# The out projection of the second two batches as seven block products per half of d_ff

## The chip, the cores and the metric

One core of one Trainium2 chip runs the whole program. The time is the device time of one launch in microseconds, the median of three runs. The work runs on five engines with instruction streams of their own: PE (matmul), DVE (elementwise with two inputs), ACT (activation, here mostly copies), POOL, and SP, which issues the DMAs.

## What is computed

Causal attention over 4 batches, 12 heads, 448 positions and head dimension 64, and then a gated product on its output:

```
x = attention(q, k, v).reshape(1792, 768)
a = x @ w_a                      # 768 x 1536
b = x @ w_b
out = (a * b) @ w_out            # 1536 x 768
```

## The kernel before

**Precision.** Every matmul operand of the gated product is split into a high part (rounded to the 4-byte matmul type) and a low part (the rest). A product of two blocks of 128 rows is three matmuls into one bank: high by high, low by high, high by low (`products`, line 629 in the profile). ACT makes the high parts (`copy`, line 284), DVE the low parts by a subtraction (`two_input`, line 300).

**Two passes.** `order` lists the work of two passes over two batches each (448 columns a batch). In the first pass, beside which the attention of batches 2 and 3 runs, every matrix goes plainly: 24 units of w_a and w_b and 12 of w_out. The second pass starts with six units `s` for the lower half of d_ff. One unit forms a 128-row block of a and of b for both batches with seven block products instead of eight, in the Winograd form of Strassen's scheme (`seven`): 7 products of 3 blocks of 3 matmuls, 63 in all. The block sums of x (T1 to T4, B11, B21, B22) lie in rooms that the attention has left (`make_rooms`), those of the weights come from `prepare_all`, four products ahead (`AHEAD`). The three PSUM banks `m` take turns; a product that adds to a bank waits until DVE or ACT has read the partial sum in it (u2, u3, c22, c21, c12 are such sums). The gated product of the unit is stored as a high and a low part in `g_hi` and `g_lo` (`part_g`).

After the six `s` units come six column blocks of w_out for this half of d_ff, for each of the two batches 6 blocks of 3 matmuls into one bank. The result of the first half is copied out of PSUM by ACT and stored to DRAM (`o_keep`); in the second half it is loaded back into an `acc` buffer, added by DVE, and stored to `out`. Then the same for the upper half of d_ff. The text calls the four stages S0, O0, S1 and O1, a unit of S by its number f = 0 to 5 in the half.

**Order.** A planner (`Plan.order`) walks a list of operations with estimated times and sets the order of every engine's stream before the program runs; among the operations that are ready on an engine it takes the one that was written first. At run time each engine keeps this order and waits on semaphores. SP's DMAs are one queue in this order.

Of the kernel before, what the change touches and what calls it, by code (L numbers as in the profile page):

```python
# [230 lines left out]
def causal_attention_then_gated_product(  # L231
# [15 lines left out]
    def sb(tag, n, shape, dt=F32):  # L247
        return plan.ring(tag, n, lambda i: sbuf.tile(shape, dt, tag=f"{tag}{i}", name=f"{tag}{i}"))
# [19 lines left out]

    v_buf = [const.tile([P, 4, 2, D], F32, name=f"v{i}") for i in range(NVB)]

# [4 lines left out]
    w_hi = const.tile([P, 18, P], F32R, name="w_hi")  # L275
    w_lo = const.tile([P, 18, P], F32R, name="w_lo")
    w_keep = [dram.tile([P, UW], F32, name=f"w_keep{u}") for u in range(NU)]
    x_keep = [[dram.tile([P, S], F32, name=f"x_keep{b}_{k}") for k in range(KT)] for b in range(2)]
# [43 lines left out]
    def convert_unit():  # L322
        u, t = w_64.pop(0)
        e, m, wt = sb("w_e", 2, [P, UW], U32), sb("w_m", 2, [P, UW], U32), sb("w_32", 3, [P, UW])

# [249 lines left out]

    raw_x = {}

# [67 lines left out]
    def convert_next():  # L645
        n = turned[0]
        turned[0] += 1
        if n < NU:
            plan.soonest = HOLD[0] + HOLD[1] * n if n <= LEAD[0] else 0.0
            convert_unit()  # L650
            plan.soonest = 0.0
            load_next()
        elif n < len(order):
            kind, f = order[n]
            if kind == "s" and f % HF == 0:
                weights[f] = [load_32(place["a"](f)), load_32(place["b"](f))]
                to_prepare[0] = prepare_all(f)
            elif kind == "o" and f >= 4:
                load_kept(in_turn[n])

    def split_next():
        n = parted[0]
        parted[0] += 1
        if n < len(order):
            kind, f = order[n]
            if kind != "s":
                split_unit()
            elif f % HF == 0:
                for _ in range(AHEAD):
                    next(to_prepare[0])  # L670

    weights, to_prepare, ready = {}, [None], []

    def prepare_all(f0):

        for f in range(f0, f0 + HF):
            a, b = weights[f]
            for i in range(7):
                if i in (0, 4):
                    if f + 1 < f0 + HF:  # L680
                        weights.setdefault(f + 1, []).append(load_32(place["ab"[i // 4]](f + 1)))
                    else:
                        load_kept(place["o"](2 * (i // 4) + f0 // HF))
# [22 lines left out]
    def seven(f, n):  # L706
# [11 lines left out]
        for i, (ps, name, first) in enumerate(plan_of):  # L718
            next(to_prepare[0], None)
            if order[n + 1][0] == "o" and i == 4:  # L720
                split_next()
            w = ready.pop(0)
# [6 lines left out]
            elif i == 1:  # L729
                u2 = sb("acc", 3, [P, S])  # L730
                added(u2, bank_b, s1)
# [3 lines left out]
            elif i == 3:  # L735
                u3 = sb("acc", 3, [P, S])
                added(u3, bank_b, s1)
# [8 lines left out]
            else:  # L746
                c12 = mid()
                added(c12, bank_c, u2)
                both(lambda: c12.t, lambda: c12.t, lambda: c22.t, ALU.mult, [c22], [c12])
                part_g(3, f, lambda: c12.t, c12)  # L750

    def uses():

        for n, (kind, f) in enumerate(order):
# [15 lines left out]
            if kind == "s":  # L770
                if order[n + 1][0] != "o":
                    split_next()
                seven(f, n)
                yield
                continue
# [150 lines left out]
```

## Time and profile before

| | us |
|---|---|
| median of 3 runs | 645.51 |
| lowest and highest run | 645.36, 646.71 |
| the profiled execution | 646.08 |
| its span, first to last instruction | 644.3 |
| PE busy in the span | 636.1 (99%) |
| DVE, ACT, POOL busy | 454.9, 347.4, 46.9 |

Busy times of one engine add up the time in which at least one of its instructions was running. Matmuls overlap one another, so a busy PE is not a measure of its speed; the distance from one start to the next is. Columns and lines are explained with the rows below. A line number names the helper that recorded the operation, so operations are told apart by the names of their tiles: `m<-x_hi,w_hi` is a matmul into bank m that streams x_hi over weights w_hi, `w_lo<-w,w_hi` the low part of a weight.

### The profile page before, as it was taken

The numbers are of one execution on the slowest core, as the hardware profiler recorded it, in microseconds if no ns is written. First come the engines' busy times: TensorE is split into PE (matmuls) and PEld (weight loads), VectorE is DVE, ScalarE is ACT, GpSimd is POOL, SyncE is SP. The second block draws the span as 40 slices with busy tenths as digits, with TensorE's granted clock in tenths as the row PEclk, the third lists the DMA queues.
The fourth block names the chain that finished last, engine by engine and source line by source line (L and its number), as shares of the span: only waits on it lengthen the run. The fifth ranks groups of instructions, "written<-read, shape, count | busy, mean of one in ns | idle before, by whom it ended". The sixth has DMA issues, their size and how long they took to land.

```text
span 644.3 us, 11138 instructions
## 1 busy us (share of the span) xinstructions
PE 636.1 (99%) x4088; PEld 565.6 (88%) x4088; DVE 454.9 (71%) x1017; ACT 347.4 (54%) x826; POOL 46.9 (7%) x104
## 2 busy tenths in 40 slices
PE   9999999999999999999999999999999999999997
PEld 6666779899889889889889889999999999999996
DVE  6799988989697396498488587687861248886421
ACT  6988648578567666666765732444432334443100
POOL 3756320000000000000000000000000000000000
PEclk9999999999999999999999999999999999999999
DMA  8636645656737466355351375222233222223532
GB/s 293 210 107 201 198 150 191 222 190 211 254 124 282 164 237 223 107 187 189 120 182 61 106 234 188 63 74 61 63 92 128 92 86 70 58 66 93 159 126 89
DMA packets 41718, 95.88 MB, mean 149 GB/s; under 512 B 4800, under 2 KB 27840, under 8 KB 41664
## 3 DMA queue, kind: packets, MB, share of 16 engines
q1 hardware_dynamic: 41664, 95.18, 44.4%
q8 instruction: 32, 0.52, 0.3%
q14 instruction: 22, 0.18, 0.1%
HBM read 67.24 MB, written 27.92 MB: 148 GB/s over the span
## 4 chain that ended last, share of the span: by engine, by line
PE 89%; DVE 7%; ACT 1%; DMA 1%; POOL 0%; issue 0%; POOLq 0%; SPq 0%; DVEq 0%
PE m L629 75%; PE t L489 5%; PE s L438 3%; PE t L438 2%; PE pv L528 1%; PE pv L509 1%; PE m L528 1%; DVE early L447 1%; DVE p L447 1%; DVE pt L292 1%; ACT early L453 1%; DVE x_lo L300 1%; PE m L438 1%; DVE w_lo L300 1%; DMA w<-w_keep 1%; DVE w_e L344 0%
## 5 line engine op out<-in xcount | busy, mean ns | idle before, releaser
L629 PE MATMUL m<-x_hi,w_hi 128*128 128x448 f32 x432 | 160.0, 370 | 0.0
L629 PE MATMUL m<-x_lo,w_hi 128*128 128x448 f32 x432 | 156.5, 362 | 0.0
L629 PE MATMUL m<-x_hi,w_lo 128*128 128x448 f32 x432 | 156.5, 362 | 0.0
L629 PE MATMUL m<-g_hi,w_hi 128*128 128x448 f32 x288 | 105.2, 365 | 0.5 <-DVE mid L300 0.5
L629 PE MATMUL m<-g_hi,w_lo 128*128 128x448 f32 x288 | 104.4, 362 | 0.0
L629 PE MATMUL m<-g_lo,w_hi 128*128 128x448 f32 x288 | 104.3, 362 | 0.0
L300 DVE TENSOR_TENSOR w_lo<-w,w_hi 128x768 fp32r<-128x768 f32 (+1 forms) x84 | 66.3, 790 | 40.2 <-ACT w_hi L284 39.5
L629 PEld LDWEIGHTS m<-x_hi,w_hi 128*128 128x128 f32 x432 | 81.1, 188 | 5.9 <-issue 0.2
L629 PEld LDWEIGHTS m<-x_hi,w_lo 128*128 128x128 f32 x432 | 81.0, 188 | 5.5
L629 PEld LDWEIGHTS m<-x_lo,w_hi 128*128 128x128 f32 x432 | 81.2, 188 | 4.9
L284 ACT ACTIVATE mid<-m 128x448 f32<-128x448 f32 x72 | 39.1, 544 | 83.0 <-PE m L629 74.4
L284 ACT ACTIVATE w_hi<-w 128x768 fp32r<-128x768 f32 (+1 forms) x84 | 59.0, 703 | 41.9 <-PE m L629 27.5
L453 ACT ACTIVATE p<-p,st 128x448 f32<-128x448 f32 (+6 forms) x126 | 62.5, 498 | 32.5 <-DVE st L447 32.0
L300 DVE TENSOR_TENSOR mid<-m,acc 128x448 f32<-128x448 f32 x48 | 29.7, 622 | 42.3 <-PE m L629 41.4
L629 PEld LDWEIGHTS m<-g_hi,w_hi 128*128 128x128 f32 x288 | 53.9, 187 | 5.5 <-DVE mid L300 1.2
L629 PEld LDWEIGHTS m<-g_lo,w_hi 128*128 128x128 f32 x288 | 54.1, 188 | 3.7
L629 PEld LDWEIGHTS m<-g_hi,w_lo 128*128 128x128 f32 x288 | 54.0, 188 | 3.3
L284 ACT ACTIVATE pt<-t 128x512 f32<-128x512 f32 x72 | 40.7, 594 | 9.4 <-PE t L489 9.3
L284 ACT ACTIVATE g_hi<-mid 128x448 fp32r<-128x448 f32 x48 | 27.6, 575 | 32.9 <-DVE mid L300 32.9
L300 DVE TENSOR_TENSOR mid<-m,mid 128x448 f32<-128x448 f32 x36 | 22.4, 622 | 28.7 <-PE m L629 21.5
L344 DVE SCALAR_TENSOR_TENSOR w_e<-w,w_e 128x768 uint32<-128x768 uint32 x36 | 34.6, 962 | 7.5 <-ACT w_e L340 7.4
L340 ACT ACTIVATE w_e<-w_e 128x768 uint32<-128x768 uint32 x36 | 30.2, 844 | 13.3 <-DVE w_e L335 12.7
(95 smaller groups left out, 1037.6 us busy)
## 6 DMA issues: line engine op xcount, KB each, us to landing
w<-w SPq DMA_DIRECT2D x36, 768.0 KB, 4.5
w_keep<-w SPq DMA_DIRECT2D x36, 384.0 KB, 3.3
w<-w_keep SPq DMA_DIRECT2D x36, 384.0 KB, 3.1
raw<-qT SPq DMA_DIRECT2D x24, 224.0 KB, 4.1
raw<-kT SPq DMA_DIRECT2D x24, 224.0 KB, 4.3
o_keep<-mid SPq DMA_DIRECT2D x24, 224.0 KB, 2.0
acc<-o_keep SPq DMA_DIRECT2D x24, 224.0 KB, 2.8
out<-mid SPq DMA_DIRECT2D x24, 224.0 KB, 2.0
```

What stands on the lines that cost most here:

```text
L284: return nc.scalar.activation(o(), i(), AF.Copy)
L292: return nc.vector.tensor_copy(o(), i())
L300: plan.op(engine, ns, lambda: e.tensor_tensor(out=o(), in0=a(), in1=b(), op=op), reads, writes)
L340: plan.op("act", 840, lambda: nc.scalar.activation(e.t, e.t, AF.Copy, bias=-896.0 * 2**23, scale=8.0), [e], [e])
L344: plan.op("dve", 900, lambda: nc.vector.scalar_tensor_tensor(out=e.t, in0=high(), scalar=0x80000000, in1=e.t, op0=ALU.bitwise_and, op1=ALU ...
L438: x = nc.tensor.matmul(at[r][0].t[to * D:(to + 1) * D, at[r][1]], q[:, r * D:(r + 1) * D], k[:, 0:D * (r + 1)], start=True, stop=True)
L447: return nc.vector.tensor_tensor_reduce(out=view(r), in0=at[r][0].t[:, at[r][1]], in1=mask[:, S - n:], scale=-0.125, scalar=3.0e38, op0=AL ...
L453: return nc.scalar.activation(view(r), view(r), AF.Exp, bias=st.t[:, nm, r:r + 1], scale=-1.0, accum_out=st.t[:, sm, r:r + 1],)
L489: x = nc.tensor.matmul(t.t[:, P * i:P * (i + 1)], p.t[:, at:at + P], swapped if r in CROSSED else ident, is_transpose=True, start=True, st ...
L509: r = nc.tensor.matmul(ps.t[j * D:(j + 1) * D, 128 * c:S], vt.t[:, c, j, :], parts[n].t[:, j, o:o + count, :].rearrange("p i d -> p (i d)" ...
L528: r = nc.tensor.matmul((ps, more)[row].t[j * D:(j + 1) * D, D * k:S], vt.t[rows, c, j, :], parts[n].t[rows, j, o:o + NR - k, :].rearrange( ...
L629: r = nc.tensor.matmul(ps.t[:, :S], a[:, i, :], x(), start=first and n == 0, stop=last and n == 2, skip_group_check=part)
```

## The change

The two passes over d_ff of the second two batches now end in three units `oo` each instead of six blocks `o`. A unit takes two column blocks of w_out and both batches and forms the four results with seven block products of 3 blocks of 3 matmuls (`seven_out`). Its operand blocks are halves of g: B11 and B21 are the first and last three blocks of the first batch, T1 the difference of the batches in the first three, B22 the last three of the second batch, and T2, T3, T4 further differences. So `seven` now stores T1 in place of the second batch's g for f = 0 to 2, and for f = 3 to 5 forms T2, T3 and T4, with their high and low parts, in rooms `pt`, `v`, `w_m`, `acc` and `raw` (`sums_room`). For that `acc` gives up one of three buffers, and the weight sums of `prepare_all` both lie in `w_e`, one buffer each. `prepare_all` runs once, over all 18 units. Each of the products' partial sums has a bank of its own (`t0`, `t1`, `s0`, `s1`, `pv`). In the second half the results of the first are loaded into the rooms x_lo and x_hi of B11 and B21 in one block of twelve loads (`keep_rooms`), and added in place. The core of the diff:

```diff
-        more = [places("pt", 3, 1, 1024) for _ in range(1)]
+        more = places("pt", 3, 2, 1024)
         block["T2"] = [one[0:3], two[0:3]]
-        block["T4"] = [[one[3], two[3], *more[0]]]
+        block["T4"] = [[one[3], two[3], more[0]]]
+        spare.append(more[1])
...
         for h in range(2):
             for f in range(h * HF, (h + 1) * HF):
                 order += [("a", f), ("b", f)] if r == 0 else [("s", f)]
-            order += [("o", 2 * e + h) for e in range(ET)]
+            if r == 1:
+                order += [("oo", NP // 2 * h + j) for j in range(NP // 2)]
+            else:
+                order += [("o", 2 * e + h) for e in range(ET)]
...
+            if n == NU:
+                units = []
+                for h in range(2):
+                    units += [(place["a"](i), place["b"](i), False) for i in range(h * HF, (h + 1) * HF)]
+                    units += [(place["o"](4 * j + h), place["o"](4 * j + 2 + h), True) for j in range(NP // 2)]
+                weights.extend([load_32(u) for u in units[0][:2]])
+                to_prepare[0] = prepare_all(units)
...
                 if i == 0:
-                    s12, s34 = (plan.ring(tag, 2, lambda j, tag=tag: sbuf.tile([P, UW], F32, tag=f"{tag}{j}", name=f"{tag}_s{j}"))
-                                for tag in ("w_e", "w_m"))
+                    s12, s34 = (plan.ring("w_e", 2, lambda j: sbuf.tile([P, UW], F32, tag=f"w_e{j}", name=f"w_e_s{j}"))
+                                for _ in range(2))
...
-                t, at = ((a, lower), (s12, upper), (a, upper), (s34, lower), (s12, lower), (b, upper), (s34, upper))[i]
+                early_six = (a, lower), (s12, upper), (a, upper), (s34, lower), (s12, lower), (b, upper), (s34, upper)
+                t, at = early_six[(0, 4, 2, 1, 3, 5, 6)[i] if late else i]
...
-                u2 = sb("acc", 3, [P, S])
+                u2 = sb("acc", 2, [P, S])
                 added(u2, bank_b, s1)
...
-                u3 = sb("acc", 3, [P, S])
+                u3 = sb("acc", 2, [P, S])
                 added(u3, bank_b, s1)
...
                 added(c12, bank_c, u2)
-                both(lambda: c12.t, lambda: c12.t, lambda: c22.t, ALU.mult, [c22], [c12])
-                part_g(3, f, lambda: c12.t, c12)
+                if f % HF < 3:
+                    t = g_raw[f % HF] = sb("raw", 4, [P, 2, S])
+                    both(lambda: t.t[:, 1], lambda: c12.t, lambda: c22.t, ALU.mult, [c12, c22], [(t, 1)])
+                    both(lambda: t.t[:, 0], lambda: t.t[:, 1], lambda: c21.t, ALU.subtract, [(t, 1), c21], [(t, 0)])
+                    part_g(3, f, lambda: t.t[:, 0], (t, 0))
+                else:
+                    k = f % HF - 3
+                    t = g_raw[k]
+                    slots = sums_room(k)
+                    both(lambda: c12.t, lambda: c12.t, lambda: c22.t, ALU.mult, [c22], [c12])
+                    for name, i, x, y in (("T2", 0, c12, None), ("T3", 1, c12, None), ("T4", 0, c21, (t, 0))):
+                        both(lambda i=i: t.t[:, i], lambda x=x: x.t, lambda i=i: t.t[:, i], ALU.subtract, [x], [(t, i)])
+                        (hi, hi_key), (lo, lo_key) = sums[name, k] = slots.pop(0), slots.pop(0)
+                        copy("act", S, hi, lambda i=i: t.t[:, i], [(t, i)], [hi_key])
+                        two_input("dve", S, lo, lambda i=i: t.t[:, i], lambda hi=hi: hi().bitcast(F32), ALU.subtract,
+                                  [(t, i), hi_key], [lo_key])
+                    part_g(3, f, lambda: c12.t, c12)
...
+    def sums_room(k):
+        if not fixed:
+            spare.extend(x for _ in range(2) for x in places("pt", 3, 2, 1024))
+            spare.extend(x for _ in range(NVB) for x in places("v", NVB, 1, 512))
+            spare.extend(over("w_m", "", 2 * UW, plan.rings["w_m"][0]))
+            spare.extend(over("acc", 2, S, plan.rings["acc"][0][2:]))
+            plan.rings["acc"] = (plan.rings["acc"][0][:2], [0])
+            fixed.extend(spare)
+        return [fixed[0:6], fixed[6:8], fixed[8:12]][k] + [x for _ in range((0, 2, 1)[k]) for x in places("raw", 4, 2, 2 * S)]
...
+    def keep_rooms():
+        for n, tag in enumerate(("x_lo", "x_hi")):
+            x = plan.ring(tag, 2, lambda i, tag=tag: sbuf.tile([P, KT, S], F32, tag=f"{tag}{i}", name=f"{tag}_o{i}"))
+            for i in range(KT):
+                kept[i // 2 * 2 + n, 2 + i % 2] = (lambda x=x, i=i: x.t[:, i, :]), (x, i)
+        for e, b in sorted(kept):
+            o, key = kept[e, b]
+            load(P * S * 4, o, lambda b=b, e=e: o_keep[b][e], [("o", b, e)], [key])
...
+    def seven_out(j):
+        h, j = divmod(j, NP // 2)
+        if h and j == 0:
+            keep_rooms()
+        banks = {name: bank(tag) for name, tag in (("1", "t0"), ("5", "t1"), ("6", "s0"), ("7", "s1"), ("4", "pv"))}
+        places_of = tuple((e, b) for e in (2 * j, 2 * j + 1) for b in (2, 3))
...
+        s1, u2, u3 = of(sb("mid", 5, [P, S])), of(sb("acc", 2, [P, S])), of(sb("acc", 2, [P, S]))
+        o11, o12, o21, o22 = (kept[p] for p in places_of) if h else (of(sb("mid", 5, [P, S])) for _ in range(4))
+        plan_of = (("1", "B11", True), ("5", "T1", True), ("1", "B21", False), ("6", "T2", True),
+                   ("7", "T3", True), ("4", "T4", True), ("5", "B22", False))
+        for i, (ps, name, first) in enumerate(plan_of):
+            ps = banks[ps]
+            next(to_prepare[0], None)
+            w = ready.pop(0)
+            for k in range(3):
+                (hi, hi_key), (lo, lo_key) = part(name, k)
+                products(ps, w, k, hi, lo, first and k == 0, k == 2, [hi_key, lo_key], True)
+            ps = of(ps)
+            if i == 0:
+                copied(s1, ps)
+            elif i == 1:
+                add(o22, o22, ps) if h else copied(o22, ps)
+            elif i == 2:
+                add(o11, o11, ps) if h else copied(o11, ps)
+                store(o11, 0)
+            elif i == 3:
+                add(u2, ps, s1)
+                if h:
+                    add(o12, o12, u2)
+            elif i == 4:
+                add(u3, ps, u2)
+                if h:
+                    add(o21, o21, u3)
+                add(o22, o22, u3)
+                store(o22, 3)
+            elif i == 5:
+                add(o21, ps, o21 if h else u3)
+                store(o21, 2)
+            else:
+                add(o12, ps, o12 if h else u2)
+                store(o12, 1)
...
+                continue
+            if kind == "oo":
+                seven_out(f)
                 yield
                 continue
```

The order of the instructions, at three places. First DVE, at the border of units 3 and 4 of a half (f = 3, 4), from the add that forms c12 out of its bank up to and with the add into u2 (`acc`) of the next unit. Names: mid holds c11, c21, c22, c12 and s1; w_e_s and w_m_s are weight sums. Before:

```order
L300 TENSOR_TENSOR mid_4961<-m_4911,acc_4887 128x448
L300 TENSOR_TENSOR g_lo<-mid_4944,g_hi 128x448
L300 TENSOR_TENSOR mid_4961<-mid_4961,mid_4931 128x448
L300 TENSOR_TENSOR w_lo<-w_4815,w_hi 128x384
L300 TENSOR_TENSOR w_e_s_4954<-w_e_s_4954,w_4874 128x384
L300 TENSOR_TENSOR w_m_s_4987<-w_4874,w_4925 128x384
L300 TENSOR_TENSOR g_lo<-mid_4961,g_hi 128x448
L300 TENSOR_TENSOR acc_4997<-m_4972,mid_4976 128x448
```

and with the change:

```order
L301 TENSOR_TENSOR mid_4932<-m_4882,acc_4860 128x448
L301 TENSOR_TENSOR g_lo<-mid_4915,g_hi 128x448
L301 TENSOR_TENSOR mid_4932<-mid_4932,mid_4902 128x448
L301 TENSOR_TENSOR w_lo<-w_4784,w_hi 128x384
L301 TENSOR_TENSOR raw_4606<-mid_4932,raw_4606 128x448 x2
L301 TENSOR_TENSOR g_lo<-mid_4932,g_hi 128x448
L301 TENSOR_TENSOR pt_x_4967<-raw_4606,pt_x_4381 128x448
L301 TENSOR_TENSOR pt_x_4974<-raw_4606,pt_x_4967 128x448
L301 TENSOR_TENSOR raw_4606<-mid_4915,raw_4606 128x448
L301 TENSOR_TENSOR acc_4986<-m_4943,mid_4947 128x448
```

Seven operations stood ahead of the one into `acc`, with the first row; ten stand now (the row with x2 is two). The weight work that stood between them, but for one row, stands behind.

Second PE, from S0 to O0. Before, the stage O0 begins with the first batch's blocks in order, right behind the last product of S0:

```order
L629 MATMUL m_5123<-x_hi_4157,w_hi 128x448
L629 MATMUL m_5123<-x_lo_4168,w_hi 128x448
L629 MATMUL m_5123<-x_hi_4157,w_lo 128x448
L629 MATMUL m_5165<-g_hi,w_hi 128x448
L629 MATMUL m_5165<-g_lo,w_hi 128x448
L629 MATMUL m_5165<-g_hi,w_lo 128x448
```

With the change the first unit's T2, whose three blocks lie in pt, v and w_m, is taken in pieces with T3 (in pt, raw, w_m and acc), behind 9 matmuls of T1 and 9 of B21:

```order
L634 MATMUL s_5220<-v_x_5082,w_hi 128x448
L634 MATMUL s_5220<-v_x_5094,w_hi 128x448
L634 MATMUL s_5220<-v_x_5082,w_lo 128x448
L634 MATMUL s_5235<-pt_x_4967,w_hi 128x448
L634 MATMUL s_5235<-pt_x_4974,w_hi 128x448
L634 MATMUL s_5235<-pt_x_4967,w_lo 128x448
L634 MATMUL s_5220<-w_m_x,w_hi 128x448 x2
L634 MATMUL s_5220<-w_m_x,w_lo 128x448
L634 MATMUL s_5235<-raw_x_5092,w_hi 128x448 x2
L634 MATMUL s_5235<-raw_x_5092,w_lo 128x448
L634 MATMUL s_5235<-w_m_x,w_hi 128x448
L634 MATMUL s_5235<-acc_x,w_hi 128x448
```

A block of T3 (bank s_5235) stands ahead of the last block of T2, so that the sum which is made last is wanted three matmuls later. B11 stands even before T4 of the last unit of S0. Likewise at f = 4 and 5 six and nine matmuls of T1 now stand ahead of T3.

Third SP, before O1. Before:

```order
L303 DMA w_5983<-w_keep_107 128x768
L303 DMA acc_5995<-o_keep_0_140 128x448
L303 DMA w_6041<-w_keep_109 128x768
L303 DMA w_6082<-w_keep_111 128x768
L303 DMA acc_6096<-o_keep_1_141 128x448
L303 DMA w_6107<-w_keep_113 128x768
L303 DMA acc_6128<-o_keep_0_146 128x448
L303 DMA w_6143<-w_keep_115 128x768
```

and with the change:

```order
L304 DMA w_6112<-w_keep_110 128x768
L304 DMA x_lo_o_6138<-o_keep_0_141 128x448
L304 DMA x_lo_o_6138<-o_keep_0_147 128x448
...
L304 DMA x_hi_o_6141<-o_keep_5_152 128x448
L304 DMA w_6210<-w_keep_112 128x768
L304 DMA w_6245<-w_keep_114 128x768
```

The loads of the first half's results stood one by one between weights and stores; now the twelve stand in a block (ten in place of the dots), ahead of the last three weight loads.

## Rows read from the trace of the kernel before

**Rows 1.** Page, the span in 40 slices: busy tenths, granted clock.

```profile
PE   9999999999999999999999999999999999999997
...
PEclk9999999999999999999999999999999999999999
...
GB/s 293 210 107 201 198 150 191 222 190 211 254 124 282 164 237 223 107 187 189 120 182 61 106 234 188 63 74 61 63 92 128 92 86 70 58 66 93 159 126 89
```

**Rows 2.** Busy time by stretch (S0, O0, S1, O1); columns in the first line.

```profile
core 0: us, PE busy (x) PEld busy (x) DVE busy (x) ACT busy (x) POOL busy (x), PEclk, DMA share, GB/s
402.78:478.38 75.60, 75.60 (x380) 70.86 (x378) 56.55 (x106) 31.26 (x62) 0.00 (x0) 1.00 0.23 68
478.38:521.58 43.20, 43.20 (x218) 40.50 (x216) 12.87 (x21) 12.20 (x22) 0.00 (x0) 1.00 0.32 111
521.58:597.18 75.60, 75.60 (x380) 70.86 (x378) 56.03 (x105) 31.70 (x63) 0.00 (x0) 1.00 0.25 73
597.18:640.38 43.20, 43.20 (x217) 40.30 (x215) 12.84 (x19) 4.15 (x6) 0.00 (x0) 1.00 0.41 129
```

**Rows 3.** The chain that ended last, its last piece: start, us, what.

```profile
386.46 254.09 PE m L629 x1269
```

**Rows 4.** Timeline of PE, first matmul of S0, O0, O1: start, us, what.

```profile
402.78 0.36 PE L629 MATMUL m<-x_hi,w_hi 128*128 128x448 f32 x1
...
478.38 0.36 PE L629 MATMUL m<-g_hi,w_hi 128*128 128x448 f32 x1
...
597.18 0.36 PE L629 MATMUL m<-g_hi,w_hi 128*128 128x448 f32 x1
```

**Rows 5.** Timeline of all engines, the end.

```profile
640.18 0.37 PE L629 MATMUL m<-g_hi,w_lo 128*128 128x448 f32 x1
640.58 0.62 DVE L300 TENSOR_TENSOR mid<-m,acc 128x448 f32<-128x448 f32 x1 [2.98 <-PE m L629]
641.23 0.33 SPq L303 DMA_DIRECT2D out<-mid  x1
```

**Rows 6.** Timeline of DVE, inside S0; in brackets idle before and its releaser.

```profile
445.53 0.56 DVE L300 TENSOR_TENSOR w_lo<-w,w_hi 128x384 fp32r<-128x384 f32 x1
446.00 0.56 DVE L300 TENSOR_TENSOR w_m_s<-w,w_e_s 128x384 f32<-128x384 f32 x1
...
449.78 0.62 DVE L300 TENSOR_TENSOR mid<-m,acc 128x448 f32<-128x448 f32 x1 [0.71 <-PE m L629]
...
453.59 0.62 DVE L300 TENSOR_TENSOR mid<-m,acc 128x448 f32<-128x448 f32 x1
454.12 0.62 DVE L300 TENSOR_TENSOR g_lo<-mid,g_hi 128x448 fp32r<-128x448 f32 x1
454.66 0.62 DVE L300 TENSOR_TENSOR mid<-mid,mid 128x448 f32<-128x448 f32 x1
```

**Rows 7.** Timeline of DVE, start of O0.

```profile
480.19 0.95 DVE L300 TENSOR_TENSOR w_lo<-w,w_hi 128x768 fp32r<-128x768 f32 x1
481.06 0.62 DVE L300 TENSOR_TENSOR g_lo<-mid,g_hi 128x448 fp32r<-128x448 f32 x1
```

**Rows 8.** Timeline of ACT, inside S1.

```profile
561.38 0.55 ACT L284 ACTIVATE mid<-m 128x448 f32<-128x448 f32 x1 [0.95 <-PE m L629]
561.82 0.57 ACT L284 ACTIVATE g_hi<-mid 128x448 fp32r<-128x448 f32 x1
562.28 0.52 ACT L284 ACTIVATE w_hi<-w_m_s 128x384 fp32r<-128x384 f32 x1
```

**Rows 9.** Page, DMA issues: count, KB each, us to landing.

```profile
w<-w_keep SPq DMA_DIRECT2D x36, 384.0 KB, 3.1
...
acc<-o_keep SPq DMA_DIRECT2D x24, 224.0 KB, 2.8
```

**Rows 10.** Busy time by stretch near the start; columns as in rows 2.

```profile
10.00:15.00 5.00, 4.98 (x61) 3.23 (x65) 5.00 (x31) 4.73 (x20) 2.98 (x7) 1.00 0.98 341
15.00:20.00 5.00, 4.42 (x44) 3.00 (x37) 3.74 (x18) 4.81 (x18) 3.66 (x9) 1.00 1.03 392
```

More of the change, by code (lines that the diff above doesn't have):

```diff
@@ L267, in causal_attention_then_gated_product @@
     p_buf = [sbuf.tile([P, PW], F32, tag=f"p{i}", name=f"p{i}") for i in range(NPB)]
-    v_buf = [const.tile([P, 4, 2, D], F32, name=f"v{i}") for i in range(NVB)]
+    v_buf = [sbuf.tile([P, 4, 2, D], F32, tag=f"v{i}", name=f"v{i}") for i in range(NVB)]
     early = sbuf.tile([P, 2 * HF * S], F32, tag="g_hi", name="early")
@@ L276, in causal_attention_then_gated_product @@
     w_lo = const.tile([P, 18, P], F32R, name="w_lo")
+    w_m = sbuf.tile([P, 2, UW], U32, tag="w_m", name="w_m")
     w_keep = [dram.tile([P, UW], F32, name=f"w_keep{u}") for u in range(NU)]
@@ L323, in convert_unit @@
         u, t = w_64.pop(0)
-        e, m, wt = sb("w_e", 2, [P, UW], U32), sb("w_m", 2, [P, UW], U32), sb("w_32", 3, [P, UW])
+        e, m, wt = sb("w_e", 2, [P, UW], U32), plan.ring("w_m", 2, lambda i: w_m[:, i]), sb("w_32", 3, [P, UW])
         def low():
@@ L574, in split_block @@
         two_input("dve", S, lo, i, lambda: hi().bitcast(F32), ALU.subtract, [key, hi_key], [lo_key])
-    raw_x = {}
+    raw_x, spare = {}, []
     def both(o, a, b, op, reads, writes):
@@ L654, in convert_next @@
             kind, f = order[n]
[L655 to L659, printed above, removed]
+            if n == NU:
[5 more added lines that the diff above has]
+                to_prepare[0] = prepare_all(units)
     def split_next():
@@ L665, in split_next, with prepare_all @@
             kind, f = order[n]
-            if kind != "s":
+            if kind not in ("s", "oo"):
                 split_unit()
-            elif f % HF == 0:
+            elif kind == "s" and f == 0:
                 for _ in range(AHEAD):
                     next(to_prepare[0])
[L672 to L677, printed above, removed]
+    weights, to_prepare, ready = [], [None], []
+    def prepare_all(units):
+        for n, (_, _, late) in enumerate(units):
+            a, b = weights.pop(0), weights.pop(0)
             for i in range(7):
                 if i in (0, 4):
[L680 to L683, printed above, removed]
+                    if n + 1 < len(units):
+                        weights.append(load_32(units[n + 1][i // 4]))
                 if i == 0:
-                    s12, s34 = (plan.ring(tag, 2, lambda j, tag=tag: sbuf.tile([P, UW], F32, tag=f"{tag}{j}", name=f"{tag}_s{j}"))
-                                for tag in ("w_e", "w_m"))
+                    s12, s34 = (plan.ring("w_e", 2, lambda j: sbuf.tile([P, UW], F32, tag=f"w_e{j}", name=f"w_e_s{j}"))
+                                for _ in range(2))
                 lower, upper = slice(0, 384), slice(384, 768)
@@ L719, in seven @@
             next(to_prepare[0], None)
-            if order[n + 1][0] == "o" and i == 4:
-                split_next()
             w = ready.pop(0)
@@ new lines, in causal_attention_then_gated_product, with over @@
+    g_raw, sums, fixed = {}, {}, []
+    def over(tag, i, width, bufs):
+        t = Buf(lambda: sbuf.tile([P, width], F32R, tag=f"{tag}{i}", name=f"{tag}{i}_x"), [u for b in bufs for u in b.users])
+        for b in bufs:
+            b.live = False
+        return [((lambda c=c: t.t[:, c * S:(c + 1) * S]), (t, c)) for c in range(width // S)]
+    def sums_room(k):
[7 more added lines that the diff above has]
+        return [fixed[0:6], fixed[6:8], fixed[8:12]][k] + [x for _ in range((0, 2, 1)[k]) for x in places("raw", 4, 2, 2 * S)]
@@ new lines, in causal_attention_then_gated_product, with part, add, of @@
+    kept = {}
+    def keep_rooms():
[12 more added lines that the diff above has]
+        places_of = tuple((e, b) for e in (2 * j, 2 * j + 1) for b in (2, 3))
+        def part(name, k):
+            if name in ("T2", "T3", "T4"):
+                return sums[name, k]
+            b, i = {"B11": (0, k), "T1": (1, k), "B21": (0, k + 3), "B22": (1, k + 3)}[name]
+            return ((lambda: g_room.t[:, b, i, :]), ("g_hi", b, i)), ((lambda: g_lo[:, b, i, :]), ("g_lo", b, i))
+        def add(o, x, y):
+            (o, o_key), (x, x_key), (y, y_key) = o, x, y
+            both(o, x, y, ALU.add, [key for key in (x_key, y_key) if key is not o_key], [o_key])
+        def of(t):
+            return (lambda: t.t[:, :S]), t
+        def copied(o, x):
+            copy("act", S, o[0], x[0], [x[1]], [o[1]], True)
+        def store(o, n):
+            e, b = places_of[n]
+            load(P * S * 4, (lambda: out[b, e]) if h else (lambda: o_keep[b][e]), o[0], [o[1]], [] if h else [("o", b, e)])
+        s1, u2, u3 = of(sb("mid", 5, [P, S])), of(sb("acc", 2, [P, S])), of(sb("acc", 2, [P, S]))
[33 more added lines that the diff above has]
+                store(o12, 1)
@@ L773, in uses @@
                 seven(f, n)
+                yield
+                continue
+            if kind == "oo":
+                seven_out(f)
                 yield
```

## Prediction

> **What bounds the kernel now.** I read the 40 slices first, then the stages of the second two batches, then the chain that ended last. PE is busy in nine tenths or more of every slice but the last, at a full granted clock (1.00 in every stage of the table) [rows 1, 2]. That alone says little, since a matmul's 0.36 us overlaps its neighbours; the chain says more: its last piece is 254.09 us of nothing but 1269 matmuls, so 0.200 us each [rows 3]. The stage borders give the same: S0 starts at 402.78, O0 at 478.38, S1 at 521.58, O1 at 597.18, and the last slot ends at 640.38 [rows 2, 4, 5]. S0 and S1 take 75.60 us for 6x63 = 378 matmuls, O0 and O1 43.20 us for 12x18 = 216: exactly 0.200 us per matmul, no slot lost. From 402.78 on PE is the only bound, so a matmul less is 0.200 us less, as long as nothing else becomes late. What could is DVE: busy 56.55 of 75.60 us in S0 and 56.03 in S1, but 12.87 and 12.84 of 43.20 in O0 and O1; ACT has 31.26 of 75.60 at most [rows 2]. In S0 DVE's timeline has idle pieces such as the 0.71 us before 449.78, ended by PE's matmul [rows 6]: DVE waits for PE there, not PE for DVE.
>
> **What goes.** A pair of column blocks takes 4x18 = 72 matmuls before and 7x9 = 63 after. Three pairs in each half: 2 x (216 - 189) = 54 matmuls, 54 x 0.200 = **10.8 us**. The order of the changed kernel has the stages at 378 and 189. The shape stays (128x448 moving, 128x128 weights), so I take the same slot. The Trainium skill (TensorE: Matmul & The Clock Gate, "Back-to-back issue gap") has about 131 ns per matmul for a stream of weight load and matmul pairs at 512 columns. An estimate by that page is 54 x 0.131 = 7.1 us and an end near 638.4; the trace does not agree, with 0.200 us at 448 columns, and I give that case no chance worth carrying.
>
> **What is added, and its cover.** Start to start, a 128x448 DVE operation takes 0.53 to 0.54 us and a 128x384 one 0.47 [rows 6], a 768-wide one 0.87 [rows 7]; on ACT 0.44 and 0.46 [rows 8].
> - S units f = 0 to 2 of a half: one more subtraction, +0.53 us of DVE. Units 3 to 5: three subtractions and three lower parts, 6 x 0.535 = +3.2 us, and three ACT copies, +1.3 us.
> - O units: 7 lower parts and 4 sums of 384, 11 x 0.47 = 5.2 us a pair (before: two of 768, 1.7 us); adds of 448: 5 a pair in O0 where ACT's copies stood, 9 in O1 where 4 stood. A pair then needs 7.9 us of DVE in O0 and 10.0 in O1 out of 12.6 us of PE. Covered, with room.
> - ACT gains 18 copies of 448 and 42 of 384 in place of 12 of 768: under 60 x 0.46 = 27.6 us, over four stages in which it was busy for 79 of 237.6 us [rows 2]. Covered. POOL has no work here, before or after.
> - An S unit: 11 x 0.47 + 9 x 0.535 = 10.0 us of DVE now, 10.5 with f = 0 to 2, **13.2 with f = 3 to 5, where PE takes 12.6**. This is the one place where cover runs out. What matters is not the sum but which wait ends last, so I walked the new order there.
>
> Place A, the border of units 3 and 4, with t = 0 at the end of unit 3's last slot. A DVE add follows its slot's end by 0.2 us (640.38 to 640.58) [rows 5]. From the add into c12 to the add into u2 ten operations now stand, seven before: 9 x 0.535 + 0.47 = 5.3, so u2 starts at 5.5 and ends (0.62 long) at 6.1. Before, it waited for PE, at 3.8. T3 overwrites nothing until u2 has read the bank; in the new order six of T1's matmuls go ahead of it, so it needs the bank at 33 slots, 6.6 us. **0.4 us of room** with 0.1 for the signal. T4 then needs u3's read: DVE reaches it at 8.6, done at 9.2, and PE asks at 48 slots, 9.6. DVE is back on time within that unit, since the work it puts off is weights that are four products ahead. Unit 5 repeats it.
>
> Place B, from S to O, t = 0 at the end of unit 5. Nothing waits for the last products' sums until T2, since B11, T1 and B21 come first. c12 starts at 0.2; eight operations later the lower part of T2's third block starts at 4.3 and ends at 4.95; PE, which runs T3's first block ahead, asks for it at 28 slots, 5.6. T4's third lower part, six operations on, ends at 8.0; PE asks for it at 43 slots, 8.6. Again about 0.5 us of room. My count is good to about 0.5 us, so each of A (twice), B in both halves, six places, may cost 0 to 0.5: 0 to 3.0 us. I take **0.5** in all, nearer to nothing because in S and O of the kernel before no slot was lost, though DVE also answered within a microsecond of being needed.
>
> - SP's queue: 12 loads of the kept halves (224 KB, as the 12 loads into acc before) now stand in one block, behind B21's last read of the room and ahead of two weight loads (384 KB). 2.75 MB at 341 GB/s, the rate of the stretch 10 to 15 us that moved tiles of the same size [rows 10], is 8.1 us, plus 1.2 for the first weight load and about 2.8 to land [rows 9]: some 12 us after B21. The first DVE operation that needs that load stands behind u2 of O1's first pair, 45 + 30 slots, 15.0 us after B21. Cover 3 us. Without it DVE would stand still with u3 and the sums behind it, and PE's next bank reads wait: at the rate of the slice average (293 GB/s at best [rows 1]) cover is still 1.5 us. Cost 0.
> - The weight sums lose one of their two buffers each: a unit's s12 waits for the last one's readers, which are two or three products (1.8 us each) older. 0. The third acc buffer goes: u2 waits for c12's add, ahead of it on DVE anyway. 0.
> - Banks t, s and pv as accumulators, and rooms v, w_m, acc: not in the trace for these matmuls; the nearest rows are those of m banks and of rooms of the same kind, with the same slot [rows 3]. 0 on either side.
> - The end: one add, one store, 640.38 to 644.30, as before [rows 5]. 0.
>
> **Sum.** The profiled execution took 646.08 us, 644.30 of span and 1.78 around it. 646.08 - 10.8 + 0.5 = 635.8; the median of the three runs is 0.57 lower, so **635.2 us**. Without any stall 634.7.
>
> **Rivals.**
> - R1, DVE is the bound in units 3 to 5: 13.2 against 12.6, 0.6 x 6 = 3.6 us, if the queue cannot be carried past a unit. 645.5 - 10.8 + 3.6 = 638.3. For it: the sum is over. Against: some 2.6 us of idle DVE time (12.6 - 10.0) in each unit before, and O's DVE nearly empty. 0.13.
> - R2, the block of 12 loads is late by a few us and DVE holds PE once: 645.5 - 10.8 + 3 = 637.7. 0.03.
> - R3, slower: DVE's idle pieces cannot be filled, because its order fixes which add waits for which slot, and each added operation lands on PE's path. 2 x (3 x 0.53 + 3 x 3.2) = 22.4, end at 657.1. It decides from 12.1 us of added waits on, so over half of that work must be exposed. Against: in the order most added operations stand where DVE was waiting for PE. 0.03.
> - R4, slower too: the new waits bring PE's clock to its lower level (1.2 GHz). One O stage at that level costs 37.8 us more, end near 672. Against it: from 15 to 20 us PE is busy 4.42 of 5.00 us and is granted 1.00 [rows 10]. The Trainium skill (same page, "A second HAM failure mode: psum-queue depth-cycling") tells of a kernel in which short idles between groups of matmuls made the clock swing. By that rule this case would come; the trace, with the clock at 1.00 beside idles of that sort, does not bear it out. 0.01.
>
> **How the numbers follow.** My forecast has 0.79, and 0.01 is left for waits that eat just the gain. A measurement of this kernel can tell about 0.2% (1.3 us) from no change. Faster: 0.79 + 0.13 + 0.03 = 0.95; same 0.01; slower 0.03 + 0.01 = 0.04. The range runs from 633.9 (no stall, and the 0.8 that runs differ from one another) to 639.0 (R1 with the same noise).
>
> **What would show it.** PE should have 54 fewer matmuls, O0 and O1 37.8 us long, S0 and S1 75.6 to 77; PE waits on DVE under 1 us after 400 us; DVE in units 3 to 5 with hardly any idle time. R1 shows as PE waits on DVE in front of T3, T4 or the O stage's T2 to T4; R2 as DVE waiting for a load near 600 us; R4 as a granted clock below 1.00. Waits above 3 us in all would make the prediction wrong.

## Result and profile after

The changed kernel takes **636.58 us** (median of 4 runs, 634.85 to 637.46) beside 646.0 us for the kernel before on the same chip (4 runs, 645.36 to 646.71): ratio 0.9851, 95% interval [0.9826, 0.9876]. It is faster, by 9.4 us, inside the range of the prediction and 1.4 us above its number.

| | before | after |
|---|---|---|
| profiled execution, us | 646.08 | 637.46 |
| its span | 644.3 | 635.4 |
| PE busy (matmuls) | 636.1 (4088) | 625.8 (4034) |
| DVE busy (instructions) | 454.9 (1017) | 511.6 (1143) |
| ACT busy | 347.4 | 367.4 |
| S0 starts, last slot ends | 402.78, 640.38 | 403.85, 631.56 |

The page's slices of the changed kernel answer to [rows 1]: PE is full to the end as before, and the clock too.

```profile
PE   9999999999999999999999999999999999999997
...
DVE  6789988989777576598597597588899768889994
...
PEclk9999999999999999999999999999999999999999
```

Busy times by stretch of the changed kernel (S0, O0, S1, O1 and the tail; columns in the first line) answer to [rows 2]:

```profile
core 0: us, PE busy (x) PEld busy (x) DVE busy (x) ACT busy (x) POOL busy (x), PEclk, DMA share, GB/s
403.85:479.60 75.75, 75.75 (x380) 71.02 (x379) 66.01 (x129) 34.80 (x71) 0.00 (x0) 1.00 0.20 61
479.60:517.40 37.80, 37.80 (x191) 35.44 (x190) 31.67 (x62) 17.49 (x36) 0.00 (x0) 1.00 0.42 137
517.40:593.00 75.60, 75.60 (x380) 70.87 (x379) 65.96 (x129) 34.70 (x71) 0.00 (x0) 1.00 0.29 89
593.00:631.50 38.50, 37.87 (x190) 35.02 (x188) 32.85 (x63) 12.29 (x24) 0.00 (x0) 1.00 0.31 113
631.50:635.40 3.90, 0.23 (x2) 0.00 (x0) 0.62 (x1) 0.00 (x0) 0.00 (x0) 1.00 0.30 115
```

(The borders are cut by hand, 0.15 us behind the slot count. PE takes B11 of an O stage ahead of the last products of S, so an S stage has no clean end.) S0 and S1 last as long as before, with 9.5 and 9.9 us more DVE work in them. O0 has gone from 43.20 to 37.80. Only O1 is too long, with PE idle for 0.63 of its 38.50. After 395 us the view of PE's waits has a single row (waiting tile and line, its releaser: us in all, times, longest):

```profile
PE t L634 <- ACT mid L285: 0.6, 1, 0.6
```

The timeline of all engines in the changed kernel at that wait, in O1's second unit (start, us, what; in brackets the idle time before and its releaser):

```profile
607.05 0.37 PE L634 MATMUL t<-g_hi,w_lo 128*128 128x448 f32 x1
...
607.42 0.55 DVE L301 TENSOR_TENSOR w_e_s<-w,w 128x384 f32<-128x384 f32 x1
607.45 0.54 ACT L285 ACTIVATE mid<-t 128x448 f32<-128x448 f32 x1 [1.48 <-PE t L634]
607.88 0.55 DVE L301 TENSOR_TENSOR w_e_s<-w,w_e_s 128x384 f32<-128x384 f32 x1
...
608.05 0.47 PE L634 MATMUL t<-g_hi,w_hi 128*128 128x448 f32 x1 [0.64 <-ACT mid L285]
...
608.35 0.55 DVE L301 TENSOR_TENSOR w_lo<-w_e_s,w_hi 128x384 fp32r<-128x384 f32 x1
608.36 0.37 PE L634 MATMUL t<-g_lo,w_hi 128*128 128x448 f32 x1
...
608.56 0.36 PE L634 MATMUL t<-g_hi,w_lo 128*128 128x448 f32 x1
...
608.82 0.62 DVE L301 TENSOR_TENSOR x_lo_o<-t,x_lo_o 128x448 f32<-128x448 f32 x1
```

B11's last matmul starts at 607.05, and the next one is B21's first, into the same bank t0, so PE stands until ACT has copied B11 out. T1 doesn't go between them: its bank t1 still holds T1 + B22 of the unit before, which DVE reads only at 608.82, behind three operations on weights. Start to start the step costs 1.00 us in place of 0.20, and the one after it 0.31: 0.80 + 0.11 = **0.91 us**. (Here and below "lost" is the sum of such excesses over 0.200 per matmul, gaps over 0.05 us.)

The rest of the spans' difference lies ahead of S0, at the end of the first pass, which has the same instructions in the same order in both kernels. Two pieces of the changed kernel's chain that ended last, beside which [rows 3] has PE's last piece begin at 386.46:

```profile
380.78 4.18 DMA w<-w_keep
385.46 0.95 DVE w_lo L301
386.41 1.08 DVE mid L301 x2
387.54 88.48 PE m L634 x441
```

and the same place in the kernel before:

```profile
380.40 3.43 DMA w<-w_keep
...
385.29 1.13 DVE mid L300 x2
```

The wait for a weight load begins 0.38 us later in the chain and is 0.75 longer; two adds that free PE's bank stand behind it on DVE. That is 1.13 us, and S0 starts 1.07 later. The account of the spans, 644.3 to 635.4: -10.8 (54 slots) + 0.91 (O1) + 1.07 (before S0) - 0.08 (tail) = -8.9.

### The profile page after: what moved, and what is told of

It is laid out like the page before. It is cut to its first block, busy times and chain, and to the rows that moved or that the text cites. A ratio compares the mean times of both kernels' runs of the same rounds, so it can differ in the third digit from the quotient of the medians.

```text
span 635.4 us, 11232 instructions
## 1 busy us (share of the span) xinstructions
PE 625.8 (98%) x4034; PEld 555.5 (87%) x4034; DVE 511.6 (81%) x1143; ACT 367.4 (58%) x874; POOL 46.9 (7%) x104
## 4 chain that ended last, share of the span: by engine, by line
PE 87%; DVE 8%; DMA 2%; ACT 1%; issue 0%; POOL 0%; SPq 0%; POOLq 0%; DVEq 0%
PE m L634 61%; PE t L634 7%; PE t L490 5%; PE s L634 3%; PE s L439 3%; PE pv L634 2%; PE t L439 2%; PE pv L510 1%; PE pv L529 1%; PE m L529 1%; DVE early L448 1%; DVE p L448 1%; DVE pt L293 1%; ACT early L454 1%; DVE x_lo L301 1%; DMA acc<-o_keep 1%
## 5 line engine op out<-in xcount | busy, mean ns | idle before, releaser
L301 DVE TENSOR_TENSOR w_lo<-w,w_hi 128x384 fp32r<-128x384 f32 (+1 forms) x90 | 64.6, 719 | 13.1 <-ACT w_hi L285 12.8
L285 ACT ACTIVATE w_hi<-w 128x384 fp32r<-128x384 f32 (+1 forms) x90 | 58.2, 648 | 27.4 <-PE m L634 12.5
L285 ACT ACTIVATE w_hi<-w_e_s 128x384 fp32r<-128x384 f32 x72 | 37.3, 522 | 52.4 <-PE m L634 30.1
L285 ACT ACTIVATE mid<-m 128x448 f32<-128x448 f32 x60 | 32.6, 544 | 52.3 <-PE m L634 52.2
L634 PE MATMUL m<-g_hi,w_hi 128*128 128x448 f32 x144 | 53.4, 371 | 1.3 <-DVE mid L301 1.2
L634 PE MATMUL m<-g_hi,w_lo 128*128 128x448 f32 x144 | 52.1, 362 | 0.0
L634 PE MATMUL m<-g_lo,w_hi 128*128 128x448 f32 x144 | 52.1, 362 | 0.0
L301 DVE TENSOR_TENSOR w_lo<-w_e_s,w_hi 128x384 fp32r<-128x384 f32 x72 | 39.7, 552 | 11.4 <-ACT w_hi L285 10.3
L467 ACT ACTIVATE p<-p,st 128x64 f32<-128x64 f32 (+6 forms) x84 | 34.9, 497 | 1.0 <-DVE st L463 1.0
L343 DVE SCALAR_TENSOR_TENSOR w_m<-w_m,w 128x768 f32<-128x768 uint32 x36 | 34.4, 954 | 0.4
```

The costliest lines, as they stand in the source:

```text
L285: return nc.scalar.activation(o(), i(), AF.Copy)
L301: plan.op(engine, ns, lambda: e.tensor_tensor(out=o(), in0=a(), in1=b(), op=op), reads, writes)
L343: plan.op("dve", 900, lambda: nc.vector.scalar_tensor_tensor(out=r(), in0=m.t, scalar=2.0**32, in1=low(), op0=ALU.mult, op1=ALU.add), [m, ...
L467: return nc.scalar.activation(view(r), view(r), AF.Copy, scale=st.t[:, rc, r:r + 1])
L634: r = nc.tensor.matmul(ps.t[:, :S], a[:, i, :], x(), start=first and n == 0, stop=last and n == 2, skip_group_check=part)
```

## Experiments

Theories before the first of them. T: a slot is worth 0.200 us, the added work is covered with some tenths to spare, and what is missing is O1's wait plus a first pass that differs from run to run. R1: DVE is the bound, so its work shows in the time. R2: the block of kept loads costs something. Runs of the kernel before that a group shared: 644.91 us (644.36 to 645.7) for e1, e2, e5 and e7; 645.47 (645.06 to 647.61) for e3, e4 and e6; 645.91 (645.3 to 646.35) for e8.

### e1_again: the changed kernel, nothing edited

> The changed kernel once more, unaltered, for a tighter interval and a second profile. Theory: 54 matmul slots of 0.200 us are saved (10.8 us) and two waits give some back: 0.9 us in O1, where B21 of the second pair stands right behind B11 and waits for ACT's copy, in every run, and 0 to 1.5 us at the end of the first pass, where DVE waits for a weight load; so 9 to 10.5 us below the kernel before, S0 and S1 at 75.6. Rival (DVE is the bound in units 3 to 5): S0 or S1 longer than 76.5 us.

635.81 us (635.43 to 636.11), 9.10 under its kernel before, ratio 0.9859 [0.9842, 0.9875]. O1's wait is there again, 0.91 us at 606.02. S0 starts at 401.82, two microseconds earlier than in the first profile of the same program, and PE has no wait between 372 and 400 us. So the 1.07 us ahead of S0 is no cost of the change: this profile and those of the kernels below have S0 at 401.6 to 402.6, and e5, which is the kernel before with nothing added, has a wait of 0.5 us at the same place. Why that load lands when it does was not looked into.

### e2_banks: other banks for T1, B11, B21, B22

```diff
-        banks = {name: bank(tag) for name, tag in (("1", "t0"), ("5", "t1"), ("6", "s0"), ("7", "s1"), ("4", "pv"))}
+        banks = {name: bank(tag) for name, tag in (("1", f"t{j % 2}"), ("6", "s0"), ("7", "s1"), ("4", "pv"))}
+        banks["5"] = m_bank()
```

> The changed kernel, with the sums of B11+B21 alternating between banks t0 and t1 by pair and those of T1+B22 in the three m banks, so that no product of a pair has to wait for the last pair's bank. Theory (the wait in O1 comes from the turn of banks at the pair's border): O1 is 37.8 us with no wait, 0.9 us less than the changed kernel. Rival (DVE is too late in O1 whatever the bank): a wait of 0.5 us or more appears at another place of O1 and the time stays.

**634.36 us** (634.11 to 635.23), ratio 0.9837 [0.9822, 0.9852]: 10.55 under its kernel before and 1.45 under e1, whose runs all lie higher. PE loses nothing from S0 on; S0's start 401.62 and 1134 slots (2 x (378 + 189)) of 0.200 give the last slot's end, 628.42. Of the 1.45, 0.91 is the wait; the rest is within what runs differ by. This version beats both kernels; e3, e4, e6 and e7 start from it.

### e8_onebank: of that, T1's bank alone

```diff
-        ... (("1", "t0"), ("5", "t1"), ("6", "s0"), ("7", "s1"), ("4", "pv"))}
+        ... (("1", "t0"), ("6", "s0"), ("7", "s1"), ("4", "pv"))}
+        banks["5"] = m_bank()
```

> Edit: of the changed kernel, only the accumulator of T1 and B22 moves, from bank t1 to one of the three banks m; B11 and B21 keep t0. Theory (the wait in O1 came of bank t1 alone: its last sum is read late by DVE, so the order had to put B21 right behind B11): no wait of PE on ACT's copy out of bank t in O1, PE loses at most 0.2 us after 400 us, 634.4 like e2_banks. Rival (B11 and B21 sharing t0 is the cause): a wait of 0.5 us or more on ACT's copy stays in O1, 635.3 or more less what the end of the first pass gives or takes.

No wait is left, and nothing is lost from S0 on. The timeline of e8 at the place where the changed kernel stood (B11's last matmul, T1's first, ACT's copy of B11, B21's first):

```profile
605.55 0.36 PE L634 MATMUL t<-g_hi,w_lo 128*128 128x448 f32 x1
...
605.75 0.36 PE L634 MATMUL m<-g_hi,w_hi 128*128 128x448 f32 x1
...
605.95 0.55 ACT L285 ACTIVATE mid<-t 128x448 f32<-128x448 f32 x1 [1.48 <-PE t L634]
...
607.55 0.36 PE L634 MATMUL t<-g_hi,w_hi 128*128 128x448 f32 x1
```

With a turn of three banks T1 (bank m) goes between B11 and B21 again, nine slots of cover for ACT's copy. B11 and B21 still share t0, so that sharing was harmless by itself; bank t1's late reader was the cause. The median, 635.56 (634.81 to 636.1, ratio 0.9844 [0.9828, 0.9861]), is 10.35 under its own kernel before, near e2's 10.55. The number expected, 634.4, was that of e2 in another group; counted from each group's own kernel before, the two agree within the spread.

### e5_less: the kernel before with 54 matmuls left out

In O0 and O1 of the kernel before, one block product of three matmuls is left out in every column block of the first of the two batches and in half of those of the second, 18 block products in all; nothing is added.

```diff
+                        if first == 2 and k == 3 and (b == 2 or h == e % 2):
+                            yield
+                            continue
```

> The kernel before, with 54 of the 432 matmuls of O0 and O1 left out (one block of three in 9 of 12 column blocks and batches of each half), so its output is not the reference's; nothing is added. It is the price of the slots alone. Theory: 10.8 us below the kernel before, O0 and O1 37.8 us long. Rival (a matmul removed is worth 0.131 us): 7.1 us below.

634.47 us (634.04 to 635.73), ratio 0.984 [0.9825, 0.9854]: 10.44 less, 10.44 / 54 = 0.193 us for a matmul. The last piece of its chain:

```profile
385.79 243.30 PE m L629 x1215
```

That is 0.2002 each. e2, with all the added work, is as fast as this kernel, which has none of it: 634.36 and 634.47 in the same group. The estimate by the Trainium skill (TensorE: Matmul & The Clock Gate, "Back-to-back issue gap"), 0.131 us a matmul or 7.1 in all, is not borne out for this 448-column, 4-byte stream.

### e3_nosums: e2 without T1 to T4

The differences of g aren't formed; the four products read blocks of g that are there (B11's, B21's and B22's parts).

```diff
-                if f % HF < 3:
...
-                else:
...
-                    for name, i, x, y in (("T2", 0, c12, None), ("T3", 1, c12, None), ("T4", 0, c21, (t, 0))):
...
+                both(lambda: c12.t, lambda: c12.t, lambda: c22.t, ALU.mult, [c22], [c12])
+                part_g(3, f, lambda: c12.t, c12)
...
+            b, i = {"B11": (0, k), "T1": (1, k), "B21": (0, k + 3), "B22": (1, k + 3),
+                    "T2": (1, k + 3), "T3": (0, k + 3), "T4": (0, k)}[name]
```

> e2_banks without the block sums of g: T1 to T4 are not formed (no subtractions, no lower parts, no copies for them), and the seven products of O0 and O1 read blocks of g that are there anyway, so the output is not the reference's. PE's work is the same, DVE has 42 operations of 0.53 us less in S0 and S1. Theory (the added DVE work is covered): the same as e2_banks, 10.3 to 10.8 us below the kernel before. Rival (DVE is the bound in units 3 to 5): 3.6 us less than e2_banks.

634.72 us (633.76 to 635.65), 10.75 under its kernel before, ratio 0.9827 [0.9809, 0.9846]. With 3 + 18 DVE operations in each half gone, 42 x 0.535 = 22.5 us of DVE, the gain over e2 (10.55) is 0.2 us, inside both intervals. The sums cost nothing. If DVE were the bound in units 3 to 5 (R1), 3.6 us would have come back.

### e4_twice and e4_thrice: where the cover ends

e2 with the lower parts of T2, T3 and T4 computed twice (18 DVE operations more, 9.6 us) and three times (36 more, 19.3 us; `range(3)` in the edit).

```diff
-                        two_input("dve", S, lo, lambda i=i: t.t[:, i], lambda hi=hi: hi().bitcast(F32), ALU.subtract,
-                                  [(t, i), hi_key], [lo_key])
+                        for _ in range(2):
+                            two_input("dve", S, lo, lambda i=i: t.t[:, i], lambda hi=hi: hi().bitcast(F32), ALU.subtract,
+                                      [(t, i), hi_key], [lo_key])
```

> e2_banks with the lower parts of T2, T3 and T4 made twice over: 3 more DVE operations (1.6 us) in each of units 3 to 5 of a half, 18 in all, so that such a unit needs 14.8 us of DVE for 12.6 of PE. It measures how near the edge the change is. Theory (room of about 0.5 us at each place and weights that can be put off by some us): 0.5 to 5 us more than e2_banks, as waits of PE on DVE in front of T3, T4 and the O stage's sums. Rival (DVE is already the bound): 18 x 0.535 = 9.6 us more.

> As e4_twice, with the lower parts of T2, T3 and T4 made three times: 36 more DVE operations, 16.4 us of DVE in a unit of 12.6 of PE. Theory (what can be put off is used up): clearly more than twice the cost of e4_twice, 6 to 17 us more than e2_banks. Rival (bound already): 19.3 us more.

Twice: 638.13 us (637.7 to 638.7), 7.34 under its kernel before, ratio 0.9881 [0.9865, 0.9897]; 3.2 of the gain are gone and PE loses 3.6 from S0 on. Three times: 647.19 (646.29 to 648.84), ratio 1.0022 [1.0009, 1.0034], so the whole gain is gone; PE loses 13.1. Waits of PE in the tripled kernel, 400 to 645 us:

```profile
PE t L634 <- DVE w_lo L301: 3.5, 2, 1.8
PE m L634 <- DVE acc L301: 2.3, 2, 1.1
...
```

The two rows on acc are place A (T3 for u2's read of the bank), once in each half; those on w_lo are B11's lower weights, behind the sums on DVE at the end of S0 and S1; two short waits in O1 are left out (0.3 and 0.2). So the change's own 22.5 us of sums cost nothing (e3), the next 9.6 us of DVE cost 3.2 and the next 9.6 nine, of which the clock's fall is about one (below). The cover was used up almost to its edge; beyond it DVE does lie on PE's path. R1's picture is right there, not in the changed kernel.

The tripled kernel also shows R4's mechanism. Its busy times around the two longest waits, one at the end of each half's S stage:

```profile
470.00:475.30 5.30, 5.30 (x28) 4.98 (x27) 5.30 (x12) 2.90 (x6) 0.00 (x0) 1.00 0.25 77
475.30:479.50 4.20, 2.38 (x11) 1.61 (x10) 4.20 (x10) 1.09 (x2) 0.00 (x0) 0.95 0.00 0
479.50:482.60 3.10, 3.10 (x10) 2.79 (x9) 3.10 (x7) 0.53 (x2) 0.00 (x0) 0.51 0.00 0
482.60:490.00 7.40, 7.40 (x39) 6.93 (x38) 6.79 (x14) 5.15 (x11) 0.00 (x0) 1.00 0.36 112
594.60:598.60 4.00, 2.17 (x10) 1.45 (x9) 4.00 (x9) 0.89 (x2) 0.00 (x0) 1.00 1.01 316
598.60:602.00 3.40, 3.40 (x10) 2.99 (x10) 3.40 (x8) 0.74 (x2) 0.00 (x0) 0.50 0.59 222
602.00:610.00 8.00, 8.00 (x41) 7.50 (x40) 7.72 (x16) 4.58 (x9) 0.00 (x0) 1.00 0.31 100
```

and its timeline of PE there:

```profile
477.47 0.48 PE L634 MATMUL t<-g_hi,w_lo 128*128 128x448 f32 x1 [1.76 <-DVE w_lo L301]
...
480.23 0.58 PE L634 MATMUL m<-pt_x,w_lo 128*128 128x448 f32 x1
480.60 0.58 PE L634 MATMUL t<-g_hi,w_hi 128*128 128x448 f32 x1
480.97 0.58 PE L634 MATMUL t<-g_lo,w_hi 128*128 128x448 f32 x1
```

About 2 us after a wait of 1.76 us, with a shorter one behind it, the granted clock goes to 0.51, the lower level of 1.2 GHz, for about 3 us, in which nine matmuls in a row start 0.37 us after the one before in place of 0.20: some 1.6 us, and as much again in the second half. That is 3.2 of the 13.1 us which PE loses in this execution, but the time shows less of it. The clock doesn't fall in every execution: the ten runs were granted 0.994 to 1.000 in the mean. The three at 0.999 and 1.000 took 646.29 to 646.69 us, the three at 0.994 and 0.995 took 647.37 to 648.84. Without the fall this kernel is thus only about a microsecond faster, and the gain is gone all the same; what takes the place of the rest was not traced. The waits of 1.15 and 1.14 us at place A in the same kernel brought no such stretch. No gap stands behind them, but that this is why is not shown.

### e6_loads: e2 with the block of kept loads issued twice

```diff
-        for e, b in sorted(kept):
+        for e, b in [x for _ in range(2) for x in sorted(kept)]:
```

> e2_banks with the twelve loads of the first half's results done twice over into the same rooms before O1, so that SP's queue has 2.75 MB more ahead of the weight loads of O1's later pairs. Theory (3 us of cover, 8 us more to move): the first DVE operation that needs the weight load behind them comes some 5 us late, holds DVE, and PE loses 1 to 5 us. Rival (the loads are off the path, other work fills the time): less than 0.3 us more than e2_banks.

634.48 us (634.39 to 635.3), 10.99 under its kernel before, ratio 0.9828 [0.981, 0.9846]: no cost, and PE loses nothing from S0 on. The loss that was expected did not come, so the cover was not what I had counted. In the changed kernel SP's queue and the first DVE operation that wants the weight load behind the block (two timelines, SP and then DVE):

```profile
585.64 0.79 SPq L304 DMA_DIRECT2D x_lo_o<-o_keep  x2
...
590.33 1.31 SPq L304 DMA_DIRECT2D x_hi_o<-o_keep  x2
592.37 4.05 SPq L304 DMA_DIRECT2D w<-w_keep  x2
```

```profile
602.87 0.55 DVE L301 TENSOR_TENSOR w_e_s<-w 128x384 f32<-128x384 f32 x1
```

The view of DMA issues has this weight load (the first of the row at 592.37), and the one at the same place in e6, by themselves; the last number is us from issue to landing:

```profile
w<-w_keep SPq DMA_DIRECT2D x1, 384.0 KB, 4.6
```

```profile
w<-w_keep SPq DMA_DIRECT2D x1, 384.0 KB, 5.1
```

The block goes out in 6 us. The weight load lands at 597.0, later after its issue than the median of 3.1 [rows 9], and the operation at 602.87 comes without a wait, 5.9 us behind the landing. In e6 eighteen of the twenty-four loads stand ahead of that weight load, it is issued at 594.18 and lands at 599.3, and DVE takes it at 601.34, again without a wait: of the 5.9 us of cover 2.0 are left.

### e7_late: e2 with weight sums later in DVE's order

A slack of 2500 ns in the planner for the sums of weights that need a fresh load, aimed at the end of the first pass, where such a sum stands ahead of two adds that PE waits for.

```diff
...
-                              [(o, at.start)])
+                              [(o, at.start)], 2500.0 if n == 0 and b in (x, y) else 0.0)
```

> As e2_banks, and the first weight sum of the second pass that needs the second weight load is planned 2.5 us later, so that two adds out of PSUM stand ahead of it on DVE. Theory (at the end of the first pass DVE's queue is held by a weight load that lands late, and PE waits for the adds behind): PE's wait on DVE near 387 us goes, 0.4 to 1.3 us less than e2_banks and less spread between runs. Rival (the lateness only moves): PE waits for weights or banks in the first unit of S0 instead, no gain.

634.48 us (634.12 to 634.69), ratio 0.9836 [0.9821, 0.9851]: no gain over e2. It decides nothing, since the load wasn't late in e2's profile either (PE has no wait between 372 and 400 us there), so there was nothing to win in these runs. Its four runs lie within 0.57 us and e2's within 1.12, too few to call it steadier.

## Why the prediction was right, and where it was off

- **What goes: 10.8 us. Right.** O0 is 37.80 long, and e5 measures 10.44 for the slots alone; every profiled stretch has them at 0.200. S0 and S1 were to be 75.6 to 77, and no slot is lost in them.
- **Places A and B, 0 to 3.0 us, 0.5 taken. They cost nothing**, but the room was smaller than I counted. Place A in the changed kernel (DVE's add into u2, then PE's T3; the unit's last slot ended at 454.25):

```profile
459.94 0.62 DVE L301 TENSOR_TENSOR acc<-m,mid 128x448 f32<-128x448 f32 x1
```

```profile
460.85 0.56 PE L634 MATMUL m<-w_x,w_hi 128*128 128x448 f32 x2
```

u2 starts at t = 5.69 (5.5 foretold) and ends at 6.31; T3 comes at 6.60 as foretold. Room 0.29 where I had 0.5 before the signal: DVE came 0.2 late to the first operation because it was still at other work, which a count that starts from the slot's end leaves out. At B of the first half T2's last lower part ended 0.49 and T4's 0.41 ahead of PE's need, where I had 0.65 and 0.6. That the walk over the order found the right places is shown in part by e4: when DVE gets more, PE stops at place A and at the S to O border. There the longest waits are for B11's lower weights, which I had not walked; T2's and T4's last lower parts stop PE too, but for less: 0.29 us for T2's and 0.14 for T4's in O1 of e4_twice. The timeline of PE there at T2's (the first row is two matmuls, of which the second waits for that part; together they last 0.85 us, where an undisturbed pair lasts 0.56):

```profile
602.05 0.85 PE L634 MATMUL s<-w_m_x,w_hi 128*128 128x448 f32 x2
...
602.74 0.37 PE L634 MATMUL s<-w_m_x,w_lo 128*128 128x448 f32 x1
```

Start to start that is 0.69 us in place of 0.40.

- **The step that was wrong is "Covered, with room" for the O stages.** I set a unit's DVE sum, 10.0 us in O1, against 12.6 us of PE and walked no order there. The sum holds nearly (32.85 busy of 38.50, so 10.95 a unit), but a wait came of one late reader: bank t1 had one buffer, its last sum of a unit is wanted by nobody but the next unit's T1, and DVE reaches it behind weight work. The step "banks t, s and pv ... 0 on either side" priced the slot of a matmul into those banks, and not what it means that t1 has one buffer where the m banks are three in turn. It measured 0.91 us. The 0.5 taken for A and B covered half of it, by chance.
- **R1 (638.3)** is out: no wait of the kind it named, and e3 gives nothing back. **R2** is out: e6. SP's block was right at 0, with 5.9 us of cover where I had 3, but my working of it was off in its parts. In PE's timeline B21's last slot in S1 starts at

```profile
585.45 0.36 PE L634 MATMUL m<-x_hi,w_lo 128*128 128x448 f32 x1
```

That slot ends at 585.65. The weight load was issued 6.7 us later, where I had 8.1, and took 4.6 to land, where I had 4.0 (1.2 and 2.8), so that it landed 11.3 us after B21, near my 12. DVE came for it 17.2 us after B21, where I had 15.0: most of the added cover is DVE being later than counted.

- **R3 (657.1)** is out: e3 has the 22.5 us of it on no path.
- **R4** is out for the changed kernel (1.00 in every stretch, also around the wait of 0.64), though the mechanism was no fancy: e4_thrice has it, after waits near three times as long. What the prediction cited from the Trainium skill (TensorE: Matmul & The Clock Gate, "A second HAM failure mode: psum-queue depth-cycling"), a clock that swings beside short idles between groups of matmuls, agrees with that run (0.51 and 0.50 behind its waits) and did not decide this case.
- **The sum.** A gain of 10.3 us was forecast (645.5 to 635.2); 9.4 was measured, and 9.1 for the same program again (e1). With O1's 0.91 in place of the 0.5 it would have been 9.9; the rest is no more than what runs differ by. With the banks in turns (e2) the kernel is at 634.36, beside the 634.7 that the prediction gave for no stall.

## What to carry to other kernels

When work is moved onto an engine with idle time, the sum over a stage tells only that it can fit; walk the order at every place where a bank or a buffer with a single copy is used again, the quiet stages included. A bank whose last reader serves nobody urgent is read late, and the next writer pays: give it a turn with others before looking for cheaper arithmetic. How near a cover is to its end is best measured by making a part of the added work twice and three times: here all of the change's own DVE work, 57 us of busy time (511.5 in e2, 454.3 in e5), was free once the banks took turns, and 19 us more cost 12.

## What the runs showed of the hardware

- A wait of PE costs more than its idle time. The first matmul after it lasts 0.47 us in place of 0.36 and the next starts 0.31 later in place of 0.20, so 0.11 us goes on top, after a wait of 0.43 us (below, e4_twice) as after one of 0.64 (the changed kernel).

```profile
475.89 0.47 PE L634 MATMUL t<-g_hi,w_lo 128*128 128x448 f32 x1 [0.43 <-DVE w_lo L301]
476.20 0.37 PE L634 MATMUL t<-g_hi,w_hi 128*128 128x448 f32 x1
```

- The granted clock stayed at 1.00 through single waits of 0.64 us (the changed kernel) and of 1.15 (e4_thrice, place A). Waits of 1.76 us with shorter ones behind them were followed by the 1.2 GHz level for some 3 us, twice in the profiled run of e4_thrice, with some 1.6 us of later starts each time. Three of the ten runs of that program were granted 0.999 or 1.000 in the mean and were about a microsecond faster.
- A weight load behind a block of others landed later than the median of its kind: 4.6 us after its issue behind twelve loads (the changed kernel) and 5.1 behind eighteen (e6), beside 3.1.
